# The first block of x in two halves, one on each hardware DMA queue

## The chip, the cores and the metric

The kernel runs on one core of one Trainium2 chip. Times are device microseconds of whole executions: three runs of the kernel before took 225.52, 225.52 and 226.03 us, so the median is 225.52 us. One further execution was taken with the hardware profiler. Its own time is 226.47 us and its span, from the first to the last instruction, is 224.7 us; 1.77 us lie around the span. All rows below are from that execution, and times in them count from the start of its span.

## What is computed

A transformer block over S = 2048 rows (tokens) of width D = 512, in bfloat16. `x` is layer-normalised once, and two branches are added to it:

```
xn  = layernorm(x)                                    # no scale, no shift
out = x + A(xn) + B(xn)

A:  q, k, v = split(xn @ wqkv)                        # 32 heads of 16
    each row s attends to rows s, s-2, ..., s-14      # 8 keys, dilation 2
    A = concat(softmax(q k / 4) v) @ wo

B:  z  = gelu(xn @ w_in)                              # width 1792, two halves of 896
    z1, z2 = z[:, :896], layernorm(z[:, 896:])
    g  = w_sp @ z2 + b_sp                             # mixes the 2048 rows
    B  = (z1 * g) @ w_out
```

## The kernel before

The 2048 rows are 16 blocks of 128 rows, one row per partition. A block of `x` is 128 x 512 bfloat16, 128 KB, in one of eight slots `("xin", slot)`. For a block, `ln_block` (from L664) issues bn_stats on VectorE (L668), bn_aggr (L671), the power that gives the reciprocal deviation on GpSimd (L673), and the normalised block (L686). Blocks 0 to 3 are then transposed by TensorE against an identity matrix (L702) and copied out of PSUM by ScalarE (L709); blocks 4 to 15 are transposed by a DMA on SP's queue (L690).

Block 0 takes a shorter way. As soon as its mean is known, its columns 256 to 511 are centred on VectorE (L676, `ctr1`) and its columns 0 to 255 on ScalarE (L678, `ctr0`, with the sign turned, which an identity with -1 takes back). TensorE transposes these (`xTr0b`, then `xTr0a`), and the product with the second half of `w_in` (`z2_0_...`, L913) begins on them; the division by the deviation is put into the gelu that reads the product (L920).

The columns 896 to 1791 of `w_in`, which `z2` needs, come in four loads (L611) of 224 KB: `w_in2a` and `w_in2b` are the two column halves, and `_0` and `_1` are rows 0 to 255 and 256 to 511. The `_0` loads are on SP's queue, the `_1` loads on ScalarE's. Block 0's product takes the rows of `_1` first.

Each engine has a list of task names in `plan.orders`, written out by hand, that fixes the order of its work; a planner puts semaphores between tasks according to what each reads and writes. The lists begin so:

```
TensorE: warm xTr0b fill0 xTr0a fill1 z2_0_0b z2_0_1b xTr1a xTr1b z2_0_0a z2_0_1a z2_1_0a ...
ScalarE: actprime ldw_in2a_1 ldw_in2b_1 ldx2 ctr0 xTe0b xTe0a xTe1a ...
VectorE: zeros steps0 steps1 bnst0 bnag0 ctr1 bnst1 bnag1 ctrB norm0 bnst2 bnag2 norm1 bnst3 norm2 ...
SP:      ldx0 ldx1 ldw_in2a_0 ldw_in2b_0 ldx3 ldx4 ldx5 ldx6 ldk ldx7 ldx10 ldx8 ldq ldx11 xTd4 ...
```

`warm` is 29 matmuls of 146 columns on constants (L640), ahead of everything else on TensorE; `fill0` and `fill1` are one and three more. `ldx4`, `ldx5`, `ldx6`, `ldx7`, `ldk` and `ldq` are made to wait until `ldw_in2b_1` has landed. `xTd4` and so on are the DMA transposes. After the first four blocks come the projections to q and k (L756), the rest of `z2` (L890) and `z1` (L933), the projection to v (L740), the mixing product with `w_sp` (L1051), and the output products (L1258, L1262).

Of the kernel before, what the change touches and what calls it, by code (L numbers as in the profile page):

```python
# [328 lines left out]
def build_kernel(nc, A_x, A_wqkv, A_wo, B_x, B_w_in, B_w_sp, B_b_sp, B_w_out, out, report=False, sched_kw=None,  # L329
# [14 lines left out]
    x2 = A_x[0]  # L344
# [75 lines left out]
    with ExitStack() as es:  # L420
# [137 lines left out]
        def dma(eng, fn, nbytes, chan, reads=(), writes=(), name="", xbar=False, prio=None, lat=1700.0):  # L558
            return T(eng, fn, reads=tuple(reads), writes=tuple(writes), name=name, prio=prio,
                     dma=dict(chan=chan, nbytes=nbytes, xbar=xbar, lat=lat))  # L560
# [10 lines left out]
          name="steps0")  # L571
        T("dve", lambda v: v.memset(FCa(foff["st6"] + 8, [[9, NB], [1, 1]]), LN_EPS * D), writes=["st_eps"], est=160,
          name="steps1")
# [5 lines left out]
          writes=["ident"], est=350, name="ident1")  # L579
# [3 lines left out]
          writes=["nident"], est=350, name="nident1")  # L583
        T("pool", lambda g: g.memset(AC(off["KT"], [[KW, 4], [1, KP]]), 0.0),
          writes=[("KTpad", c, 0) for c in range(4)], est=200, name="ktpad", prio=2)
# [15 lines left out]
        def xin_ap(sl):  # L601
            return A("xin", 512, 512 * sl) if sl < 4 else A("xin2", 512, 512 * (sl - 4))

        def ld_x(b, eng="sp", after=()):
            sl = b % 8
            dma(eng, lambda e: e.dma_start(xin_ap(sl), x2[128 * b:128 * b + 128, :]), 128 * 512 * 2,
                ("xin", sl), reads=after, writes=[("xin", sl)], name="ldx%d" % b)
# [7 lines left out]

        ld_x(0)
        ld_x(1)
# [4 lines left out]
        for which, eng in ((0, "sp"), (1, "sp")):  # L622
# [4 lines left out]
                writes=[(("wq", "wk")[which], c) for c in range(4)],  # L627
                name="ld%s" % ("qk"[which]))
# [7 lines left out]
        def filler(n, name, est, prio=None, reads=(), w=512):  # L636
# [10 lines left out]
          est=-1200, name="actprime", tbl="gelu")  # L647
# [16 lines left out]
        def ln_block(b):  # L664
            sl = b % 4
            xs_ = b % 8
            xin = xin_ap(xs_)
            T("dve", lambda v: v.bn_stats(Fv("st6", 6, 9 * b), xin),  # L668
              reads=[("xin", xs_)], writes=[("st6", b)],
              est=690, name="bnst%d" % b)  # L670
            T("dve", lambda v: v.bn_aggr(Fv("mv", 2, 2 * b), Fv("st6", 9, 9 * b)), reads=[("st6", b), "st_eps"],  # L671
              writes=[("mv", b)], est=180, name="bnag%d" % b)
            T("pool", lambda g: g.tensor_tensor(Fv("rstd", 1, b), Fv("mv", 1, 2 * b + 1), Fv("mhalf", 1), ALU.pow),  # L673
              reads=[("mv", b), "mhalf"], writes=[("rstd", b)], est=580, name="rstd%d" % b)
            if b == 0:
                T("dve", lambda v: v.tensor_scalar(A("attn", 256, 256), xin[:, 256: 512], Fv("mv", 1, 2 * b), None, ALU.subtract),  # L676
                  reads=[("xin", xs_), ("mv", b)], writes=[("xc", 1)], est=250, name="ctr1")
                T("act", lambda a: a.activation(A("attn", 256), xin[:, 0: 256], ACTF.Identity, bias=Fv("mv", 1, 2 * b),  # L678
                                                scale=-1.0),
                  reads=[("xin", xs_), ("mv", b)], writes=[("xc", 0)], est=400, name="ctr0")  # L680
            if b == 1:
# [3 lines left out]
            xk = "xn0" if b == 0 else ("xn", sl)  # L685
            T("dve", lambda v: v.tensor_scalar(AC(xo, [[1, 512]]), xin, Fv("mv", 1, 2 * b),  # L686
                                               Fv("rstd", 1, b), ALU.subtract, ALU.mult),
              reads=[("xin", xs_), ("mv", b), ("rstd", b)], writes=[xk], est=400, name="norm%d" % b)
            if b >= XDMA:
# [588 lines left out]
        for t in range(NT):  # L1278
# [11 lines left out]
            if t >= 1:  # L1290
# [17 lines left out]
            """  # L1308
                actprime ldw_in2a_1 ldw_in2b_1 ldx2 ctr0 xTe0b xTe0a xTe1a xTe1b z2g0_0 z2g0_1 xTe2a xTe2b xNe xTe3a
                xTe3b z2g1_0 xNeB z2g1_1 z2g2_0 z2g3_0 z2g3_1 z2g2_1 QKe0_0 z2s0 QKe0_1 QKe0_2 QKe0_3 z2s1 QKe1_0 z2s2  # L1310
# [33 lines left out]
            """  # L1344
                ldx0 ldx1 ldw_in2a_0 ldw_in2b_0 ldx3 ldx4 ldx5 ldx6 ldk ldx7 ldx10 ldx8 ldq ldx11 xTd4 xTd5 xTd6 xTd7
                ldx9 ldx14 ldx13 ldx12 xTd10 xTd11 ldx15 xTd8 xTd9 ldwv xTd14 ldb xTd12 xTd13 xTd15 ldw_in1 w0_1 w0_0
# [56 lines left out]
```

## Time and profile before

| | |
|---|---|
| three runs | 225.52, 225.52, 226.03 us |
| profiled execution, its own time | 226.47 us |
| its span | 224.7 us |
| TensorE busy | 220.6 us, 98% of the span |
| VectorE busy | 207.8 us, 92% |
| ScalarE busy | 135.0 us, 60% |
| GpSimd busy | 89.7 us, 40% |
| moved by DMA | 29.96 MB, 133 GB/s on average |

In the rows, PE is TensorE, PEld its weight loads, DVE VectorE, ACT ScalarE, POOL GpSimd. SPq and ACTq are the DMA-issuing instructions of SP and ScalarE. "L913 PE MATMUL ... x10" is ten matmuls of line 913 that follow each other; the first number is the start of the first one, the second the time until the last one ends. A matmul's end is modelled, and the next one starts before it. In the chain of work, each piece is followed back to what released it, and the pieces follow each other without overlap.

### The profile page before, as it was taken

What the parts mean: (1) busy time and instruction counts of PE and PEld (TensorE: products, weight loads), DVE (VectorE), ACT (ScalarE), POOL (GpSimd) and SP (SyncE); (2) the same over time, 40 slices, a digit from 0 to 9 for tenths busy, and PEclk for the clock granted to TensorE, in tenths of its full rate; (3) what the DMA queues carried; (4) which work ended last, traced back from release to release, by engine and by line L of the source; (5) the groups of instructions that cost most, each with busy time, mean ns of one, the idle gap of its engine ahead of it and who ended that gap; (6) DMA issues with size and microseconds to landing.
All of it is one profiled execution on the core that took longest, in us unless ns stands there. A gap on an engine that the chain in (4) does not pass through costs nothing.

```text
span 224.7 us, 3133 instructions
## 1 busy us (share of the span) xinstructions
PE 220.6 (98%) x1170; PEld 123.3 (55%) x1184; DVE 207.8 (92%) x237; ACT 135.0 (60%) x242; POOL 89.7 (40%) x38
## 2 busy tenths in 40 slices
PE   8999999999999999999999999999999999999995
PEld 7555555554577776665555454544545444444544
DVE  4798999999999999999999999999999999999810
ACT  4679899999999999986343304424404216224442
POOL 3454568985000081000000799955999910000000
PEclk9999999999999999999999999999999999999999
DMA  6895442590000002879779997849989697328352
GB/s 218 266 171 140 94 119 50 122 263 13 3 0 0 0 0 46 213 179 204 183 141 179 228 148 154 180 127 179 187 165 221 137 171 175 98 61 176 111 113 93
DMA packets 77716, 29.96 MB, mean 133 GB/s; under 512 B 68731, under 2 KB 75401, under 8 KB 77702
## 3 DMA queue, kind: packets, MB, share of 16 engines
q1 hardware_dynamic: 74566, 25.08, 55.3%
q10 hardware_dynamic: 3136, 4.69, 6.3%
q8 instruction: 9, 0.15, 0.3%
q14 instruction: 5, 0.04, 0.1%
HBM read 9.05 MB, written 2.10 MB: 50 GB/s over the span
## 4 chain that ended last, share of the span: by engine, by line
PE 97%; DMA 1%; DVE 1%; issue 0%; ACT 0%
PE ps L1051 38%; PE ps L756 12%; PE ps L933 11%; PE ps L1262 11%; PE ps L890 8%; PE ps L740 6%; PE ps L1258 6%; PE ps L913 3%; DMA arena<-in_A_x_dram 1%; PE ps L814 1%; PE ps L702 1%; DVE fpool L668 0%; PE ps L640 0%; PE ps L724 0%; DVE arena L676 0%
## 5 line engine op out<-in xcount | busy, mean ns | idle before, releaser
L1051 PE MATMUL ps<-arena 128*128 128x448 f16 (+1 forms) x448 | 86.7, 352 | 0.0
L873 POOL TENSOR_TENSOR arena<-arena,fpool 128x128 bf16<-128x128 f32 x2 | 49.9, 24944 | 45.7 <-DVE arena L869 45.7
L1051 PEld LDWEIGHTS ps<-arena 128*128 128x128 f16 (+1 forms) x448 | 43.8, 98 | 41.4
L779 DVE TENSOR_TENSOR arena<-arena 128x8192 bf16<-128x8192 bf16 (+1 forms) x10 | 35.6, 3556 | 0.8 <-ACT arena L764 0.8
L1196 DVE TENSOR_TENSOR arena<-arena 128x4096 bf16<-128x4096 bf16 x16 | 36.2, 2282 | 0.0
L962 POOL TENSOR_TENSOR fpool<-fpool 128x4 f32<-128x4 f32 x4 | 18.1, 4538 | 27.3 <-DVE fpool L959 27.3
L756 PE MATMUL ps<-arena 128*128 128x512 bf16 x124 | 27.7, 379 | 0.2
L1200 DVE TENSOR_TENSOR arena<-arena 128x4096 bf16<-128x4096 bf16 (+1 forms) x16 | 27.9, 1745 | 0.0
L1066 ACT ACTIVATE ps<-ps 128x448 f32<-128x448 f32 x16 | 8.4, 527 | 32.2 <-PE ps L1051 24.7
L1262 PE MATMUL ps<-arena 128*128 128x512 bf16 (+2 forms) x125 | 27.1, 355 | 0.1
L787 DVE TENSOR_TENSOR arena<-arena 128x4096 bf16<-128x4096 bf16 (+1 forms) x9 | 26.9, 2992 | 0.1
L933 PE MATMUL ps<-arena 128*128 128x448 bf16 x128 | 24.7, 352 | 0.0
L673 POOL TENSOR_TENSOR fpool<-fpool 128x1 f32<-128x1 f32 x16 | 17.5, 1094 | 17.0 <-DVE fpool L671 16.7
L1069 ACT ACTIVATE arena<-ps,fpool 128x448 bf16<-128x448 f32 x16 | 10.0, 636 | 22.6 <-PE ps L1051 22.6
L933 PEld LDWEIGHTS ps<-arena 128*128 128x128 bf16 x128 | 18.5, 144 | 5.9
L756 PEld LDWEIGHTS ps<-arena 128*128 128x128 bf16 x128 | 14.5, 113 | 13.0 <-issue 0.2
L1271 ACT ACTIVATE arena<-ps 128x512 bf16<-128x512 f32 (+2 forms) x17 | 9.4, 563 | 16.7 <-PE ps L1262 16.7
L890 PE MATMUL ps<-arena 128*128 128x448 bf16 x96 | 19.2, 353 | 0.0
L1262 PEld LDWEIGHTS ps<-arena 128*128 128x128 bf16 x126 | 11.9, 98 | 12.4
L764 ACT ACTIVATE arena<-ps 128x1024 bf16<-128x1024 f32 x16 | 16.1, 1026 | 2.5 <-PE ps L756 2.4
L1258 PE MATMUL ps<-arena 128*128 128x512 bf16 (+2 forms) x65 | 15.3, 353 | 0.4
L945 ACT ACTIVATE arena<-arena 128x896 bf16<-128x896 bf16 x16 | 15.3, 955 | 0.0
(87 smaller groups left out, 260.1 us busy)
## 6 DMA issues: line engine op xcount, KB each, us to landing
arena<-in_A_x_dram ACTq DMA_DIRECT2D x8, 256.0 KB, 3.3
arena<-in_A_x_dram SPq DMA_DIRECT2D x15, 128.0 KB, 2.5
out_dram<-arena ACTq DMA_DIRECT2D x7, 256.0 KB, 2.4
arena<-in_A_wqkv_dram SPq DMA_DIRECT2D x3, 512.0 KB, 4.3
arena<-in_B_w_in_dram SPq DMA_DIRECT2D x1, 896.0 KB, 5.4
arena<-in_B_w_out_dram SPq DMA_DIRECT2D x1, 896.0 KB, 5.1
arena<-arena SPq DMA_DIRECT2D x2, 448.0 KB, 4.5
arena<-arena SPq DMA_DIRECT2D x1, 672.0 KB, 5.6
```

The source lines that it names most:

```text
L756: last = t.matmul(bank(k + which), AC(off["wqk"] + 1024 * dc + col0, [[4, 128]]), AC(off["xnT"] + dc * S + 512 * j, [[1, 512]]), start=(dc ...
L779: T("dve", lambda v: v.tensor_tensor(pbv, qb, kb, ALU.mult), reads=[(t_, c, j) for t_ in ("QT", "KT", "KTpad") for c in cs], writes=[("pb" ...
L787: T("dve", lambda v: v.tensor_tensor(av, av, bv, ALU.add), reads=[("pb", s_) for s_ in b], writes=[("pb", s_) for s_ in a], est=c_dve(4096 ...
L873: T("pool", lambda g: g.tensor_tensor(Rv, Zv, FCa(foff["mone"], [[0, 128]]), ALU.pow), reads=[kz, "mone"], writes=[kr], est=20000, name="s ...
L890: last = t.matmul(ps[:, 512 * (k + hf): 512 * (k + hf) + HF], AC(off["xnT"] + dc * S + 128 * b, [[1, 128]]), AC(off["w_in2"] + FH * dc + H ...
L933: lastm = t.matmul(ps[:, 512 * (k + hf): 512 * (k + hf) + HF], AC(off["xnT"] + dc * S + b, [[NTOK, 128]]), AC(off["w_in1"] + FH * dc + HF ...
L962: T("pool", lambda g: g.tensor_tensor(Fv("rstd2", 4, 4 * j), Fv("msq", 4, 4 * j), mhalf, ALU.pow), reads=[("msq", j), "mhalf"], writes=[(" ...
L1051: last = t_.matmul(pb_(k_), st(k), mv(k), start=(start and k == 0), stop=(k == 7), skip_group_check=True)
L1196: T("dve", (lambda iv, tv, av: lambda v: v.tensor_tensor(tv, iv, av, ALU.mult))(iv, tv, av), reads=[("attn", q // 4)] + [("V", i_) for i_ ...
L1200: T("dve", (lambda n: lambda v: v.tensor_tensor(AC(off["Vs"], [[4096, 2], [1, n]]), AC(off["Vs"], [[4096, 2], [1, n]]), AC(off["Vs"] + n, ...
L1258: t_.matmul(po, AC(off["OT"] + 1024 * (t % 3) + 512 * r_ + 128 * cc, [[1, 128]]), AC(off["wo"] + 512 * cc + c0, [[1, n]]), start=False, st ...
L1262: last = t_.matmul(po, AC(off["z1"] + FH * tb + 128 * fc, [[1, 128]]), AC(off["w_out"] + 512 * fc + c0, [[1, n]]), start=False, stop=(fc = ...
```

## The change

Block 0 of `x` is no longer one load of 128 rows on SP's queue. It becomes two loads of 64 rows, 64 KB each: `ldx0a`, rows 0 to 63, stays first on SP's queue, and `ldx0b`, rows 64 to 127, goes to ScalarE's queue, ahead of the two weight loads there. Each half has its own semaphore, and what reads block 0 depends on both.

```
-        ld_x(0)
+        for h in range(2):
+            dma(("sp", "act")[h], (lambda h: lambda e: e.dma_start(xin_ap(0)[64 * h: 64 * h + 64, :], x2[64 * h: 64 * h + 64, :]))(h),
+                64 * 512 * 2, (("xin", 0), "xin0b")[h], writes=[(("xin", 0), "xin0b")[h]], name="ldx0%s" % "ab"[h])
         ld_x(1)
...
             T("dve", lambda v: v.bn_stats(Fv("st6", 6, 9 * b), xin),
-              reads=[("xin", xs_)], writes=[("st6", b)],
+              reads=[("xin", xs_)] + (["xin0b"] if b == 0 else []), writes=[("st6", b)],
...
     plan.orders, ScalarE:
-                actprime ldw_in2a_1 ldw_in2b_1 ldx2 ctr0 xTe0b xTe0a xTe1a ...
+                actprime ldx0b ldw_in2a_1 ldw_in2b_1 ldx2 ctr0 xTe0b xTe0a xTe1a ...
     plan.orders, SP:
-                ldx0 ldx1 ldw_in2a_0 ldw_in2b_0 ldx3 ...
+                ldx0a ldx1 ldw_in2a_0 ldw_in2b_0 ldx3 ...
```

`ctr1`, `ctr0` and `norm0` also name `xin0b` among what they read. The order of all other instructions on all engines stays what it was.

More of the change, by code (lines that the diff above doesn't have):

```diff
@@ L676, in ln_block @@
                 T("dve", lambda v: v.tensor_scalar(A("attn", 256, 256), xin[:, 256: 512], Fv("mv", 1, 2 * b), None, ALU.subtract),
-                  reads=[("xin", xs_), ("mv", b)], writes=[("xc", 1)], est=250, name="ctr1")
+                  reads=[("xin", xs_), "xin0b", ("mv", b)], writes=[("xc", 1)], est=250, name="ctr1")
                 T("act", lambda a: a.activation(A("attn", 256), xin[:, 0: 256], ACTF.Identity, bias=Fv("mv", 1, 2 * b),
                                                 scale=-1.0),
-                  reads=[("xin", xs_), ("mv", b)], writes=[("xc", 0)], est=400, name="ctr0")
+                  reads=[("xin", xs_), "xin0b", ("mv", b)], writes=[("xc", 0)], est=400, name="ctr0")
             if b == 1:
@@ L687, in ln_block @@
                                                Fv("rstd", 1, b), ALU.subtract, ALU.mult),
-              reads=[("xin", xs_), ("mv", b), ("rstd", b)], writes=[xk], est=400, name="norm%d" % b)
+              reads=[("xin", xs_), ("mv", b), ("rstd", b)] + (["xin0b"] if b == 0 else []), writes=[xk], est=400, name="norm%d" % b)
             if b >= XDMA:
@@ L1308, in build_kernel @@
             """
-                actprime ldw_in2a_1 ldw_in2b_1 ldx2 ctr0 xTe0b xTe0a xTe1a xTe1b z2g0_0 z2g0_1 xTe2a xTe2b xNe xTe3a
+                actprime ldx0b ldw_in2a_1 ldw_in2b_1 ldx2 ctr0 xTe0b xTe0a xTe1a xTe1b z2g0_0 z2g0_1 xTe2a xTe2b xNe xTe3a
                 xTe3b z2g1_0 xNeB z2g1_1 z2g2_0 z2g3_0 z2g3_1 z2g2_1 QKe0_0 z2s0 QKe0_1 QKe0_2 QKe0_3 z2s1 QKe1_0 z2s2
@@ L1344, in build_kernel @@
             """
-                ldx0 ldx1 ldw_in2a_0 ldw_in2b_0 ldx3 ldx4 ldx5 ldx6 ldk ldx7 ldx10 ldx8 ldq ldx11 xTd4 xTd5 xTd6 xTd7
+                ldx0a ldx1 ldw_in2a_0 ldw_in2b_0 ldx3 ldx4 ldx5 ldx6 ldk ldx7 ldx10 ldx8 ldq ldx11 xTd4 xTd5 xTd6 xTd7
                 ldx9 ldx14 ldx13 ldx12 xTd10 xTd11 ldx15 xTd8 xTd9 ldwv xTd14 ldb xTd12 xTd13 xTd15 ldw_in1 w0_1 w0_0
```

## The prediction

> **What bounds the kernel now.** I read the page's busy times first, then the chain of work, then the chain in order of time, where the share of each engine can be put into a place.
>
> ```profile
> PE 220.6 (98%) x1170; PEld 123.3 (55%) x1184; DVE 207.8 (92%) x237; ACT 135.0 (60%) x242; POOL 89.7 (40%) x38
> ...
> PE 97%; DMA 1%; DVE 1%; issue 0%; ACT 0%
> ```
>
> ```profile
> 0.74 0.07 issue
> 0.80 2.55 DMA arena<-in_A_x_dram
> ...
> 3.38 0.70 DVE fpool L668
> ...
> 4.11 0.21 DVE fpool L671
> ...
> 4.34 0.30 DVE arena L676
> 4.63 0.14 issue
> 4.77 0.37 PE ps L702 x2
> ...
> 5.93 1.26 PE ps L913 x4
> 7.19 0.22 PE ps L702 x4
> 7.42 1.89 PE ps L913 x10
> ...
> 13.61 0.05 issue
> 13.66 10.74 PE ps L756 x49
> ```
>
> From 4.77 us to the end the chain is TensorE alone, with pieces of 0.05 us between. Only the first 4.77 us are something else: the load of block 0 (2.55 us from its issue at 0.80), then bn_stats, bn_aggr and the centring on VectorE. The change works on that head. What it can take away is therefore bounded by the load's part of 4.77 us, and everything behind must move forward with it.
>
> Two things stand between an earlier load and an earlier end. The first is what TensorE does meanwhile; the second is its pace. The timeline of the first microseconds, TensorE and the DMA issues:
>
> ```profile
> 0.84 3.69 PE L640 MATMUL ps<-const-bfloat16-1.0 128*128 128x146 bf16 x29 [0.84 <-PEq L1388]
> 4.77 0.37 PE L702 MATMUL ps<-arena 128*128 128x128 bf16 x2 [0.24 <-DVE arena L676]
> 4.93 0.42 PE L640 MATMUL ps<-const-bfloat16-1.0 128*128 128x256 bf16 x1
> ...
> 5.72 1.47 PE L913 MATMUL ps<-arena 128*128 128x448 bf16 x4
> ...
> 7.25 2.06 PE L913 MATMUL ps<-arena 128*128 128x448 bf16 x10
> ```
>
> ```profile
> 0.80 0.88 SPq L606 DMA_DIRECT2D arena<-in_A_x_dram  x2
> ...
> 0.94 0.95 ACTq L611 DMA_DIRECT2D arena<-in_B_w_in_dram  x2
> ...
> 1.72 0.95 SPq L611 DMA_DIRECT2D arena<-in_B_w_in_dram  x2
> ...
> 1.92 0.49 ACTq L606 DMA_DIRECT2D arena<-in_A_x_dram  x1
> ```
>
> The 29 filler matmuls stand ahead of block 0 in TensorE's order and last until 4.53 us by their modelled end; TensorE is idle for only 0.24 us before the first transpose. Whatever the load gains beyond about that is spent waiting for the fillers. A next matmul may start before the modelled end of the last (L640 at 4.93, 0.21 us ahead of 4.77 + 0.37), so I put this cap at 0.24 to 0.45 us.
>
> As to the pace: the first L913 matmuls follow each other at 0.37 us (the 1.47 us of four, less one's overlap, and 1.26 / 4 = 0.315 in the chain, where the step is inside), the next ten at 1.89 / 10 = 0.189 us. The form is the same, so TensorE doubles its pace at about 6.9 us, though the page prints a granted clock of full speed in every slice. If that step keeps its place in time, an earlier start by s buys only s / 2, because the time won is spent at half pace.
>
> **What the load of block 0 waits for.** Busy time in stretches of 0.5 us; the last two columns are the DMA engines' busy share and GB/s:
>
> ```profile
> 1.50:2.00 0.50, 0.50 (x6) 0.50 (x5) 0.00 (x0) 0.50 (x1) 0.35 (x3) 1.00 0.21 66
> 2.00:2.50 0.50, 0.50 (x7) 0.50 (x6) 0.00 (x0) 0.29 (x2) 0.24 (x2) 1.00 0.75 203
> 2.50:3.00 0.50, 0.50 (x7) 0.50 (x6) 0.00 (x0) 0.00 (x0) 0.00 (x0) 1.00 0.91 273
> 3.00:3.50 0.50, 0.50 (x7) 0.50 (x6) 0.12 (x1) 0.00 (x0) 0.00 (x0) 1.00 1.08 373
> ```
>
> By 2.5 us 0.5 x (66 + 203) = 134 thousand bytes have moved, as much as block 0 holds, but block 0 lands only at 3.35. So part of what moved was not block 0: its tail shares the DMA engines with the first weights on ScalarE's queue, issued 0.14 us after it. What a load of this size takes with emptier engines shows in block 4's, issued at 5.5 us:
>
> ```profile
> L606 SPq DMA_DIRECT2D arena<-in_A_x_dram x1: 340/340/340, 5.5 to 5.5; - x1
> ...
> DMA to landing us min/median/max: 2.0/2.0/2.0
> ```
>
> **The change, part by part.** *The first half on SP.* It has the place of the whole load (issue at 0.80 us) and half its packets, so it lands no later than 3.35 us; it isn't the later half, and costs nothing. Its issue is one instruction as before (0.88 / 2 = 0.44 us), so SP's next loads keep their times.
>
> *The second half on ScalarE's queue.* It takes the first place there, at 0.94 us. No row shows a load of 64 rows. Bounds: with block 4's 2.0 us it lands at 2.94; with block 0's own 2.55 us, as crowded as now, at 3.49, which is 0.14 us later than today. I take 3.05 us, close to the first, because the weights that crowded the load are now behind it on its own queue, and only block 1 on SP's queue (issued 0.44 us behind the first half) can get between. That is 0.30 us earlier. Bn_stats, bn_aggr and centring follow at their own durations, with VectorE idle before them, so they move by the same 0.30.
>
> *TensorE.* The first transpose moves by the smaller of 0.30 and the cap; I take 0.27. The centring on ScalarE and the copies out of PSUM move along, as ScalarE is idle there. At half pace until about 6.9 us that is 0.13 us of gain, at full pace 0.27.
>
> *ScalarE's other loads.* One more issue of 0.95 / 2 = 0.48 us stands ahead of `w_in2a_1`, `w_in2b_1` and block 2. Their times to landing, in this order:
>
> ```profile
> L611 ACTq DMA_DIRECT2D arena<-in_B_w_in_dram x1: 432/432/432, 0.9 to 0.9; - x1
> ...
> DMA to landing us min/median/max: 3.0/3.0/3.0
> ```
>
> ```profile
> L611 ACTq DMA_DIRECT2D arena<-in_B_w_in_dram x1: 488/488/488, 1.4 to 1.4; - x1
> ...
> DMA to landing us min/median/max: 4.1/4.1/4.1
> ```
>
> ```profile
> L606 ACTq DMA_DIRECT2D arena<-in_A_x_dram x1: 489/489/489, 1.9 to 1.9; - x1
> ...
> DMA to landing us min/median/max: 4.3/4.3/4.3
> ```
>
> They land at 3.9, 5.5 and 6.2 us now, and at most 0.48 us later then: 4.4, 6.0 and 6.7. The first is needed by the first L913, at 5.72 - 0.27 = 5.45: cover 1.0 us. The second is needed by the third L913, two matmuls of 0.37 later: 6.2 us, cover 0.2 us, the thinnest on TensorE. The third feeds the third bn_stats, which has no cover at all:
>
> ```profile
> 6.21 0.69 DVE L668 BATCH_NORM_STATS2 fpool<-arena 128x6 f32<-128x512 bf16 x1
> ...
> 7.95 0.40 DVE L686 TENSOR_SCALAR arena<-arena,fpool 128x512 bf16<-128x512 bf16 x1
> ...
> 18.15 2.29 DVE L779 TENSOR_TENSOR arena<-arena 128x4096 bf16<-128x4096 bf16 x1 [0.82 <-ACT arena L764]
> ```
>
> ```profile
> L702 PE MATMUL ps<-arena x4: 219/219/219, 9.1 to 9.3; 128*128 128x128 bf16 x4
> ```
>
> VectorE then runs up to 0.5 us late: block 2 is normalised at 8.35 + 0.5 = 8.85 us, and TensorE transposes it at 9.1 - 0.2 = 8.9: just covered. VectorE's lateness ends at 18.15 us, where it waits 0.82 us for ScalarE today.
>
> *SP's later loads* wait for `w_in2b_1`:
>
> ```profile
> SPq L606 <- DMA arena<-in_B_w_in_dram: 2.4, 1, 2.4
> ```
>
> Blocks 4 to 7 and the weights of q and k come up to 0.5 us later. Block 4 lands at 5.5 + 2.0 = 7.5 us and is wanted by VectorE only behind block 3's work, after the L686 row of 7.95, so 0.5 is about covered. I cost it at nothing.
>
> **The sum**, against the profiled execution's own 226.47 us (1.77 us around the span don't change): 226.47 - 0.13 to 0.27 = 226.2 to 226.34. The three runs have their median 0.95 us below the profiled execution; the same difference taken from the median gives 225.52 - 0.13 to 0.27. I say **225.35 us**, 0.1% less. Under 0.3% (0.68 us) a measurement of this kernel can't be told from no change.
>
> **A rule of the skill against the change.** The trace shows both queues in flight at once: the weights that ScalarE issued at 0.94 land at 3.9, block 0 at 3.35. The Trainium skill, DMA: Bandwidth & Descriptors, Rules for kernel authors, says of two transfers to disjoint halves of the partitions that one should not bother: both spread over the same 16 DMA engines and serialise. By that rule splitting alone wins nothing; the rows leave room for the other part, the place ahead of the weights.
>
> **The rivals.** *No gain.* The halves finish no sooner than the whole did. For it: the same engines serve both queues, and block 1 follows the first half on SP's queue as the weights followed before. Against: 0.21 and 0.75 busy shares while block 0 moves. Landing at 3.49 it costs 0.14 us at full pace, 0.07 at half: 225.6 us.
>
> *A larger gain, through the pace.* The 0.24 us gap before the first transpose closes; if the step in pace comes with unbroken work, it comes earlier. Had it come where the fillers end, at 4.53 instead of 6.9 us, 2.4 us at half pace would be 1.2 us less, plus the full 0.27: 224.1. Halfway, 224.7. For it: the runs differ by 0.51 us among themselves, as a step that isn't tied to the program would make them. Against: that gap didn't prevent the step now. The Trainium skill, TensorE: Matmul & The Clock Gate, The HAM clock gate, says that the clock doubles after a busy window of about 3.4 us and that this window runs free of the kernel. By that rule the gap hardly matters and the step's place is chance; the trace agrees in the doubling, and one execution can't show the rest.
>
> *Slower: a hole in TensorE's work just before the step.* `w_in2b_1` lands after 6.2 us, because SP's queue has weights of its own in flight from 1.72 us on. By itself the wait costs what it lasts, 0.3 us where it lands at 6.5, as SP's second weight load does today. It decides only where the hole delays the step in pace: the fillers took 6.9 - 0.84 = 6.1 us of work to reach it, so the price runs from half the hole to half of 6.1 us, 3.0 us; in the middle 1.5 us: 226.9 us. For it: cover of 0.2 us only. Against: part of the DMA traffic ahead of it is lighter by the half that left SP's queue.
>
> **How the numbers follow.** Forecast (225.1 to 225.5) 0.46; no gain (225.5 to 225.7) 0.18; larger gain through the pace (224.1 to 224.9) 0.20; slower 0.16. The first two and the spread of the runs (225.52 to 226.03) fall within 0.3%, but for a little: faster 0.22, same 0.62, slower 0.16. The range leaves out the slower case and the lower end of the larger gain: 224.5 to 226.1 us; for the forecast alone 225.0 to 225.8.
>
> **What would show it.** In the profile after: the wait of L668 for block 0 shorter by 0.3 us (1.97 us now); TensorE's idle time before its first L702 gone or below 0.1 us; the first L913 at about 5.45 us; third bn_stats later than 6.21 us and nobody on TensorE waiting for it; the pace still doubling near 6.9 us. The prediction is wrong if block 0 lands at 3.35 or later, if L913 waits for a weight load, or if the step in pace moves.

## The result, and the profile after

Eleven runs of the changed kernel have their median at 227.23 us (lowest 227.04), eleven runs of the kernel before beside them at 225.87 us (lowest 225.38). The ratio is 1.0074, with a 95% interval of 1.0049 to 1.0099: the change makes the kernel 0.7% slower, where 0.1% faster was predicted. Two of the eleven runs (228.88 and 228.90 us), and three of the six of e14 below (229.43 to 229.77), had a granted clock of 0.992 to 0.993 and took some 1.7 us longer than the others; without them the medians are 227.22 us here, 0.6% above the kernel before, and 227.72 us in e14. The profiled execution took 227.11 us, with a span of 225.4 us; before, these were 226.47 and 224.7.

In the page, the shares of the chain that ended last have moved. Only the first row of that part is shown:

```profile
PE 93%; DMA 2%; ACT 1%; DVE 1%; ACTq 1%; issue 0%
```

Before, 97% was TensorE. The chain in order of time (start, duration, what) shows what came in:

```profile
1.52 0.78 ACTq L611
...
2.34 0.49 ACTq L611
...
2.86 4.70 DMA arena<-in_A_x_dram
...
7.58 0.70 DVE fpool L670
...
9.40 0.33 DVE arena L688
9.72 0.05 issue
9.77 0.40 PE ps L704 x4
...
14.29 0.81 PE ps L758 x3
```

The chain no longer starts with block 0. It goes through the two weight issues on ScalarE's queue to the load of block 2, issued at 2.86 us, which takes 4.70 us to land at 7.56. The third bn_stats (L670, before: L668) starts at 7.58, and the third group of transposes (L704, before: L702) at 9.77. Before, the same three stood at 6.2, 6.21 and 9.15. The projections (L758, before: L756) start at 14.29 instead of 13.66: 0.63 us, and the spans differ by 0.7.

TensorE and VectorE in their timelines (in brackets the idle time before, and what ended it):

```profile
4.71 0.40 PE L704 MATMUL ps<-arena 128*128 128x128 bf16 x2 [0.19 <-DVE arena L678]
...
6.01 0.78 PE L915 MATMUL ps<-arena 128*128 128x448 bf16 x2
6.94 0.55 PE L915 MATMUL ps<-arena 128*128 128x448 bf16 x2 [0.15 <-DMA arena<-in_B_w_in_dram]
7.33 0.39 PE L704 MATMUL ps<-arena 128*128 128x128 bf16 x4
7.55 2.06 PE L915 MATMUL ps<-arena 128*128 128x448 bf16 x10
9.77 0.40 PE L704 MATMUL ps<-arena 128*128 128x128 bf16 x4 [0.16 <-DVE arena L688]
```

So the first transpose is 0.06 us earlier (4.71, before 4.77), the first product is 0.29 us later (6.01, before 5.72), and two waits have appeared, one for `w_in2b_1` at 6.94 and one for block 2 at 9.77. TensorE's waits in the first 14 us add a third, of its weight loads, for the first product:

```profile
PEld ps L915 <- DMA arena<-in_B_w_in_dram: 0.8, 1, 0.8
```

The lateness begins with the issues of SP and ScalarE (start, duration):

```profile
0.80 0.59 SPq L617 DMA_DIRECT2D arena<-in_A_x_dram  x1
1.45 0.56 SPq L606 DMA_DIRECT2D arena<-in_A_x_dram  x1
2.06 0.95 SPq L611 DMA_DIRECT2D arena<-in_B_w_in_dram  x2
```

```profile
0.94 0.55 ACTq L617 DMA_DIRECT2D arena<-in_A_x_dram  x1
1.52 0.79 ACTq L611 DMA_DIRECT2D arena<-in_B_w_in_dram  x1
2.34 0.49 ACTq L611 DMA_DIRECT2D arena<-in_B_w_in_dram  x1
2.86 0.49 ACTq L606 DMA_DIRECT2D arena<-in_A_x_dram  x1
```

A half takes 0.59 and 0.55 us to issue, where the whole of block 0 and the first weights took 0.40 and 0.43. The next weight issue takes 0.79. ScalarE's three loads are therefore issued 0.58, 0.93 and 0.94 us later than before (1.52, 2.34 and 2.86 against 0.94, 1.41 and 1.92), and SP's weights 0.34 us later (2.06 against 1.72). What the halves themselves got for it shows in the view of their line (times from issue to landing):

```profile
L617 ACTq DMA_DIRECT2D arena<-in_A_x_dram x1: 547/547/547, 0.9 to 0.9; - x1
...
DMA to landing us min/median/max: 2.2/2.3/2.4
```

One half lands 2.2 us after 0.80, the other 2.4 us after 0.94, at 3.3. The whole block landed at 3.35. Nothing was won there: bn_stats for block 0 starts at 3.41 us (3.38 before). In the trace it starts 0.10 us behind the later half's landing, at 3.31; before, it started 0.02 us behind the landing. So it is in all executions below: 0.10 us where block 0 comes in two loads, 0.02 where it comes in one, and the few hundredths that the halves win are lost in this. And the DMA engines started late. Stretches of 0.5 us as in the prediction, the last number GB/s:

```profile
1.50:2.00 0.50, 0.50 (x6) 0.50 (x5) 0.00 (x0) 0.50 (x1) 0.35 (x3) 1.00 0.00 0
2.00:2.50 0.50, 0.50 (x7) 0.50 (x6) 0.00 (x0) 0.29 (x2) 0.24 (x2) 1.00 0.44 135
2.50:3.00 0.50, 0.50 (x7) 0.50 (x6) 0.00 (x0) 0.00 (x0) 0.00 (x0) 1.00 0.86 225
3.00:3.50 0.50, 0.50 (x7) 0.50 (x6) 0.09 (x1) 0.00 (x0) 0.00 (x0) 1.00 1.00 226
3.50:4.00 0.50, 0.50 (x7) 0.50 (x5) 0.50 (x1) 0.00 (x0) 0.00 (x0) 1.00 0.81 156
...
4.50:5.00 0.50, 0.31 (x4) 0.25 (x4) 0.50 (x2) 0.38 (x1) 0.50 (x1) 1.00 1.08 369
5.00:5.50 0.50, 0.50 (x7) 0.48 (x5) 0.46 (x2) 0.35 (x1) 0.07 (x1) 1.00 1.10 380
```

Before, the first four of these moved at 66, 203, 273 and 373 GB/s, and the fifth was:

```profile
3.50:4.00 0.50, 0.50 (x7) 0.50 (x6) 0.50 (x1) 0.00 (x0) 0.00 (x0) 1.00 1.13 372
```

The late start is the smaller part: by 2.5 us 0.07 MB are missing, and 0.18 MB more from 3.0 to 4.0 us. The DMA view from 1.5 to 5 us adds it up, first for the kernel before, then for the changed one:

```profile
DMA packets 1143, 1.00 MB, mean 285 GB/s; under 512 B 75, under 2 KB 1143, under 8 KB 1143
```

```profile
DMA packets 815, 0.70 MB, mean 200 GB/s; under 512 B 70, under 2 KB 815, under 8 KB 815
```

By 5 us 0.30 MB less has come in. At the 369 to 380 GB/s that the changed kernel moves from 4.5 us on, that is 0.8 us by which the stream of first loads is behind. Block 2 and `w_in2b_1` are later than that, by 1.4 us: on ScalarE's queue 64 KB more stand ahead of them. At half of 375 GB/s these would take 0.35 us, an estimate; the rest isn't explained.

### The profile page after: what moved, and what is told of

Its sections match the earlier page's. It is cut to its first block, busy times and chain, and to the rows that moved or that the text cites. A ratio compares the mean times of both kernels' runs of the same rounds, so it can differ in the third digit from the quotient of the medians.

```text
span 225.4 us, 3135 instructions
## 1 busy us (share of the span) xinstructions
PE 220.9 (98%) x1170; PEld 122.9 (55%) x1184; DVE 207.8 (92%) x237; ACT 135.0 (60%) x242; POOL 89.7 (40%) x38
## 3 DMA queue, kind: packets, MB, share of 16 engines
q10 hardware_dynamic: 3216, 4.75, 6.4%
## 4 chain that ended last, share of the span: by engine, by line
PE 93%; DMA 2%; ACT 1%; DVE 1%; ACTq 1%; issue 0%
PE ps L1053 38%; PE ps L758 12%; PE ps L935 11%; PE ps L1264 11%; PE ps L892 8%; PE ps L742 6%; PE ps L1260 6%; DMA arena<-in_A_x_dram 2%; PE ps L816 1%; PE ps L915 1%; DVE fpool L670 1%; ACTq L611 1%; ACT arena L922 1%; ACT L648 0%; PE ps L704 0%
## 5 line engine op out<-in xcount | busy, mean ns | idle before, releaser
L758 PE MATMUL ps<-arena 128*128 128x512 bf16 x124 | 27.7, 379 | 0.2
L758 PEld LDWEIGHTS ps<-arena 128*128 128x128 bf16 x128 | 14.5, 113 | 13.0
```

The lines of the kernel that those rows point to most:

```text
L758: last = t.matmul(bank(k + which), AC(off["wqk"] + 1024 * dc + col0, [[4, 128]]), AC(off["xnT"] + dc * S + 512 * j, [[1, 512]]), start=(dc ...
```

## The experiments

Where the profiles had left the question: TensorE waits both for `w_in2b_1` (call it W: the loss is made by late weights) and for block 2 (call it X: the loss is made by late x), and either could come from the issue at the head of ScalarE's queue, from the 64-row form, or from the bytes on the shared engines. The first four kernels take the parts of the change one at a time, the next four tell W from X, the next four price block 2 and other orders, the last three ask whether late data is all there is. Ratios are to runs of the kernel before on the same chip; e8 and e15 are single runs. In the table (e13 and e14 are in the text), "projections" is the start of the first projection matmul in the profiled execution, "rest" is its span less that start.

| run | median us | ratio to before, 95% | first transpose | projections | span | rest |
|---|---|---|---|---|---|---|
| before (prediction's) | | | 4.77 | 13.66 | 224.7 | 211.0 |
| e8 before again | one, 226.10 | | 4.79 | 13.08 | 224.4 | 211.3 |
| after | 227.23 | 1.0074 [1.0049, 1.0099] | 4.71 | 14.29 | 225.4 | 211.1 |
| e15 after again | one, 226.96 | | 4.75 | 14.14 | 225.2 | 211.1 |
| e1 both halves on SP | 227.37 | 1.0062 [1.0050, 1.0074] | 5.78 | 14.56 | 225.6 | 211.0 |
| e2 whole at ScalarE's head | 227.55 | 1.0060 [1.0043, 1.0077] | 4.74 | 14.73 | 225.9 | 211.2 |
| e3 half of block 1 there | 226.70 | 1.0043 [1.0028, 1.0058] | 4.40 | 13.76 | 224.8 | 211.0 |
| e4 4 KB there | 226.84 | 1.0039 [1.0025, 1.0053] | 4.33 | 14.52 | 225.6 | 211.1 |
| e5 after, no w_in2 needed | 227.29 | 1.0056 [1.0042, 1.0069] | 4.75 | 14.27 | 225.6 | 211.3 |
| e6 before, no w_in2 needed | 226.06 | 1.0008 [0.9995, 1.0020] | 4.65 | 14.06 | 225.4 | 211.3 |
| e7 block 1 and weights exchanged | 225.85 | 0.9994 [0.9983, 1.0006] | 4.68 | 12.81 | 224.1 | 211.3 |
| e9 blocks 2 and 3 exchanged | 226.34 | 1.0025 [1.0014, 1.0035] | 4.68 | 13.52 | 224.6 | 211.1 |
| e10 halves by columns | 226.81 | 1.0045 [1.0031, 1.0059] | 4.32 | 14.32 | 225.6 | 211.3 |
| e11 as e5, block 2 first | 227.08 | 1.0055 [1.0033, 1.0076] | 4.78 | 14.20 | 226.2 | 212.0 |
| e12 block 2 and weights exchanged | 226.19 | 1.0012 [1.0003, 1.0021] | 4.70 | 13.48 | 224.6 | 211.1 |

The last column is the main reading: but for e11 the rest is 211.0 to 211.3 us, whatever was done to the first loads. What differs between these kernels is over by the first projection, and all of it is when TensorE gets there. The first transpose's column doesn't go with it. Each of these columns is one execution, and the kernel before alone has its projections at 13.08 and at 13.66; a single row of them proves little, and the ratios rest on the medians. Nor can a difference under 0.3 us in the projections be read as one in time, as the rest varies by that much.

**e1: the split without the second queue.** Both halves on SP's queue, ScalarE's as before.

```
-            dma(("sp", "act")[h], ... ldx0a/ldx0b
+            dma("sp", ...
     ScalarE:  actprime ldw_in2a_1 ldw_in2b_1 ldx2 ...
     SP:       ldx0a ldx0b ldx1 ldw_in2a_0 ldw_in2b_0 ldx3 ...
```

> Both halves of block 0 on SP's queue, one behind the other; ScalarE's queue as in the kernel before. Theory Q (the extra load at the head of ScalarE's queue pushes the first weights back, which leaves holes in TensorE's work): the weights on ScalarE's queue land near 3.9 and 5.5 us again, the first L915 is at 5.7 us, and the time is within 0.3% of the kernel before. Theory H (a load of 64 rows is itself dear to issue, 0.55 to 0.59 us against 0.40, and starts the transfers late): SP's loads come 0.8 us later than before, block 0 lands no sooner than 3.3 us, and the time is 0.3 to 0.7% above the kernel before.

The issues take 576 and 592 ns, with 128 rows' 398 before. The weights are in time, but the second half of block 0 lands 2.9 us after its issue, at 4.4:

```profile
L617 SPq DMA_DIRECT2D arena<-in_A_x_dram x2: 576/584/592, 0.8 to 1.4; - x2
...
DMA to landing us min/median/max: 2.6/2.7/2.9
```

The first transpose moves to 5.78 us. H has its time, and Q's "within 0.3%" failed. So the split alone, with no load added to ScalarE's queue, costs as much as the change, by another route: on one queue the second half is late, on two queues everything else is.

**e2: the move without the split.** Block 0 whole, 128 rows, at the head of ScalarE's queue; SP begins with block 1.

```
-        ld_x(0)
+        ld_x(0, "act")
     ScalarE:  actprime ldx0 ldw_in2a_1 ldw_in2b_1 ldx2 ...
     SP:       ldx1 ldw_in2a_0 ldw_in2b_0 ldx3 ...
```

> Block 0 whole (128 rows) at the head of ScalarE's queue; SP starts with block 1. No load of 64 rows. Theory Q: 128 KB and one issue ahead of the weights on ScalarE's queue; w_in2a_1 lands at 5 us or later, w_in2b_1 at 6.3 us or later, 0.4 to 0.8% slower than the kernel before. Theory H: issues of 0.4 to 0.49 us, transfers start at 1.85 to 2.0 us, the weights land at most 0.5 us later than before (4.4 and 6.0), within 0.3% of the kernel before.

Issues of 128 rows take 0.38 to 0.40 us on both queues. Block 0 is no earlier, and TensorE waits for `w_in2b_1`:

```profile
7.37 0.55 PE L913 MATMUL ps<-arena 128*128 128x448 bf16 x2 [1.20 <-DMA arena<-in_B_w_in_dram]
```

The loss is the same size as the change's without any 64-row load, as Q expected and H didn't: a load put ahead of the first weights is enough. But in this execution the stream is hardly behind: 0.95 MB have moved by 5 us, against 1.00 before. The trace has 16 increments of a semaphore for each of these loads, and the last one is the landing. Fifteen of `w_in2b_1`'s come by 6.25 us and the last at 7.32; of block 2's, by 6.87 and at 8.00. One part in sixteen is late here, not all.

**e3 and e4: what one more issue there costs.** In e3 block 0 stays whole on SP, and the second half of block 1 takes the place at ScalarE's head. In e4 a load of 4 KB that is needed late (`b_sp`) takes it.

```
e3   ScalarE:  actprime ldx1b ldw_in2a_1 ldw_in2b_1 ldx2 ...      SP:  ldx0 ldx1a ...
e4   ScalarE:  actprime ldb ldw_in2a_1 ldw_in2b_1 ldx2 ...        SP:  ldx0 ldx1 ... (ldb left out)
```

> Block 0 stays whole and first on SP's queue; block 1 is split instead, its second half at the head of ScalarE's queue. Block 0 no longer plays a part in the split. Theory Q: w_in2a_1 lands after 5 us, w_in2b_1 after 6.5 us, 0.4 to 0.8% slower than the kernel before, like the change. Theory H: SP's first issue is 0.40 us again and only ScalarE's is 0.55 us; transfers start at 1.83 us; slower by 0.2 to 0.4%.

> The kernel before with a load of 4 KB (b_sp, which SP loads later otherwise) at the head of ScalarE's queue: one more issue there, next to no bytes. Theory Q in its pure form (the issue alone counts): weights 0.45 us later or more, w_in2a_1 at 4.4 us or later, and 0.2 to 0.5% slower. If it is the bytes ahead of the weights, or the 64 rows, that count: w_in2a_1 lands by 4.5 us and the time is within 0.2% of the kernel before.

Both get block 0 early, which the change was to do and didn't: with the first weights issued 0.58 and 0.42 us later, the whole load of 128 rows lands at 3.1 and 3.0 us, without being split. The first transposes follow at 4.40 and 4.33 without idle time before them, at the cap that the fillers set. Both are still 0.4% slower, as Q had it, though e3's weights land at 4.8 and 6.0 us, earlier than Q expected. In e3:

```profile
6.06 0.55 PE L915 MATMUL ps<-arena 128*128 128x448 bf16 x2 [0.34 <-DMA arena<-in_B_w_in_dram]
...
9.24 0.40 PE L704 MATMUL ps<-arena 128*128 128x128 bf16 x4 [0.43 <-DVE arena L688]
```

Even 4 KB ahead of the weights costs 0.9 us (it comes in small packets, 204 under 512 B by 5 us against 75 before, so this isn't the price of an issue alone). An earlier block 0 is worth nothing as long as the loads behind it are late.

**e5 and e6: W against X.** In both, the product (L915, before: L913) of blocks 0 to 3 reads a tile of zeros where it read `w_in2`, so that it doesn't wait for the weights; e5 does that to the changed kernel, e6 to the one before.

```
-   t.matmul(ps[...], st, AC(off["w_in2"] + FH * dc + c0, [[1, HF]]), ...
-   reads=[..., (wk_, h)]
+   t.matmul(ps[...], st, A("zeros", HF), ...
+   reads=[..., "zeros"]
```

> The changed kernel, but the z2 products of blocks 0 to 3 (L915) read a tile of zeros, which is ready at 1.2 us, in place of the columns of w_in that the four first weight loads bring; these loads are still issued, and all other work is as it was (the output's z2 of these blocks is not computed). So L915 can't wait for a weight load. Theory W (the late weights make the loss): the time falls to the kernel before or below, at most 0.2% above it. Theory X (block 2 of x, late behind the weights on ScalarE's queue, makes the loss through the third bn_stats and the third transpose): the wait of L704 for VectorE near 9.7 us stays, grows to about 0.8 us, and the kernel stays 0.4% or more slower than the kernel before.

> The same edit in the kernel before, as the control (z2 of blocks 0 to 3 is not computed from w_in). No theory has TensorE waiting for the weights there, so the time is that of the kernel before within 0.2%. If it is faster by 0.3% or more, the weights held TensorE before the change as well.

The wait for weights is gone in e5, and the time is not better: 1.0056. TensorE is ahead and gives it all back before the third transposes, for which block 2 isn't there (TensorE, then VectorE):

```profile
6.50 2.06 PE L915 MATMUL ps<-arena 128*128 128x448 bf16 x10
9.96 0.40 PE L704 MATMUL ps<-arena 128*128 128x128 bf16 x4 [1.40 <-DVE arena L688]
```

```profile
7.77 0.69 DVE L670 BATCH_NORM_STATS2 fpool<-arena 128x6 f32<-128x512 bf16 x1 [1.52 <-DMA arena<-in_A_x_dram]
```

So W isn't needed for the loss, and X is sufficient. The control is unchanged in time (1.0008). Its profiled execution happens to be the slowest of its twelve, 227.09 us against the median of 226.06, and shows the same hole from the other side: there block 2 came late by itself, third bn_stats at 7.57 us after a wait of 1.41 us, and TensorE waited 1.29 us. A late block 2 thus costs about 1 us in a kernel without the change too. Its loads and their issues are those of the kernel before, and 0.95 MB have moved by 5 us. What is late is again one part: fifteen of block 2's increments come by 5.82 us, as in the prediction's profile (5.86), and the last at 7.54 instead of 6.19. Meanwhile the DMA share (the number before the last) is about one engine in sixteen:

```profile
6.50:7.00 0.50, 0.50 (x6) 0.23 (x3) 0.00 (x0) 0.50 (x2) 0.00 (x0) 1.00 0.07 25
7.00:7.50 0.50, 0.50 (x4) 0.27 (x3) 0.00 (x0) 0.50 (x2) 0.00 (x0) 1.00 0.07 23
```

In the changed kernel it is different: all sixteen increments of block 2 come from 6.74 to 7.56 us, the first of them later than the last before. Why a part falls behind in e2 and e6, no run here shows.

**e7: an order that should keep both in time.** Block 1 heads ScalarE's queue, and `w_in2a_1` goes behind block 0 on SP's.

```
     ScalarE:  actprime ldx1 ldw_in2b_1 ldx2 ...
     SP:       ldx0 ldw_in2a_1 ldw_in2a_0 ldw_in2b_0 ldx3 ...
```

> The kernel before with two loads exchanged one for one: block 1 heads ScalarE's queue, and w_in2a_1 follows block 0 on SP's. The number of issues on each queue stays. If block 0's load is held up by what heads the other queue, block 0 lands at 3.0 to 3.2 us instead of 3.35 and TensorE's first transpose is at 4.4 to 4.6 us instead of 4.77. By the theory that an extra issue on ScalarE's queue makes the loss, nothing is lost: w_in2b_1 lands at 5.5 us, block 2 at 6.2 us, time equal or 0.1 to 0.2% faster. If the bytes ahead of each load decide, w_in2a_0 and w_in2b_0 land 0.3 us later, still in time.

Block 0 lands at 3.27 (3.0 to 3.2 was expected of a load that is held up by the other queue's first), and the third bn_stats is at 6.28: nothing late, nothing won, 0.9994. It adds no issue to either queue, and it is the only reordering here that costs nothing.

**e8: the kernel before, once more.**

> The kernel before once more, for a second trace. If the landing times are set by the program, block 0 lands at 3.35 us within 0.1, the weights at 3.9 to 6.6 us within 0.2, and block 2 at 6.2 us. If the step in TensorE's pace falls at another moment, the span differs by up to 1 us with the same landings.

With the same order and the same loads, four products now take 1.08 us where they took 1.47 in the prediction's profile, and the projections start at 13.08 instead of 13.66:

```profile
5.75 1.08 PE L913 MATMUL ps<-arena 128*128 128x448 bf16 x4
```

The doubling of TensorE's pace comes some 0.7 us earlier, at about 6.1 us instead of 6.8. The execution took 226.10 us, 0.37 less than the prediction's 226.47, about half of 0.7. So a late step is part of why the medians differ by 1.36 us and the two first profiles by only 0.64, and not all of it. The landings weren't all where they were expected: block 0's was, at 3.4, but `w_in2b_1` landed at 4.9 us instead of 5.5 and block 2 at 5.8 instead of 6.2.

**e9: block 2 late alone.** Blocks 2 and 3 exchange queues, so that block 2 comes last on SP's.

```
     ScalarE:  actprime ldw_in2a_1 ldw_in2b_1 ldx3 ...
     SP:       ldx0 ldx1 ldw_in2a_0 ldw_in2b_0 ldx2 ldx4 ...
```

> The kernel before with blocks 2 and 3 of x exchanged between the queues: block 2 is the last of SP's first loads (block 3 landed there at 6.9 us), block 3 is on ScalarE's queue. Block 0 and all weights as before. It measures the price of block 2's lateness alone. Theory X (block 2 sets the end): it lands 0.7 us later, at 6.9 us, TensorE's third transpose waits for VectorE by 0.3 to 0.7 us and the kernel is 0.15 to 0.35% slower (0.3 to 0.8 us). If block 2's landing doesn't matter below 7.5 us: within 0.1% of the kernel before.

Here nothing is split and nothing added. Block 2 is 0.6 us later than in the prediction's profile:

```profile
6.81 0.69 DVE L668 BATCH_NORM_STATS2 fpool<-arena 128x6 f32<-128x512 bf16 x1 [0.71 <-DMA arena<-in_A_x_dram]
```

TensorE waits 0.42 us before the third transposes, and the median is 226.34 against 225.77, 0.57 us. The late block has the price that X gives it.

**e10: the halves by columns.** Both halves have 128 rows of 512 bytes, on the two queues, in the change's order.

```
-   xin_ap(0)[64 * h: 64 * h + 64, :],      x2[64 * h: 64 * h + 64, :]
+   xin_ap(0)[:, 256 * h: 256 * h + 256],   x2[0:128, 256 * h: 256 * h + 256]
```

> The change with another cut: each half is all 128 rows and half of the columns (512 bytes a row), on the same queues at the same places. Theory H (64 rows are dear to issue): the two issues take 0.40 us instead of 0.55 to 0.59, transfers start at 1.85 us instead of 2.1, block 2 lands at 6.6 to 7.0 us instead of 7.56, and the kernel is 0.2 to 0.45% slower than the kernel before instead of 0.6 to 0.75%. If the extra load on ScalarE's queue alone makes the loss: the same landings and time as the change, 0.6% or more.

With 128 rows an issue of 64 KB takes 0.39 and 0.38 us, and both halves have landed 1.9 and 2.0 us after it:

```profile
L617 ACTq DMA_DIRECT2D arena<-in_A_x_dram x1: 384/384/384, 0.9 to 0.9; - x1
...
DMA to landing us min/median/max: 1.9/2.0/2.0
```

Block 0 is complete at 2.9 us, 0.4 us earlier than whole: in this form the step that was predicted does happen, the first transpose is at 4.32, and the kernel is 0.45% slower all the same. Most of that step needs no halves: in e4, with the weights as late, the whole load lands at 3.0. TensorE waits 0.36 and 0.25 us for weights and 0.61 us for block 2. H has its issues and its time, but not its reason: block 2 lands at 7.6 us, as in the change, and not at 6.6 to 7.0, and 0.73 MB have moved by 5 us. The halves of 512-byte rows have the stream as late as the halves of 64 rows.

**e11: the changed kernel with block 2 in time.** As e5, with block 2 directly behind the second half on ScalarE's queue, ahead of the weights that aren't needed there.

```
     ScalarE:  actprime ldx0b ldx2 ldw_in2a_1 ldw_in2b_1 ...
```

> The changed kernel with the tile of zeros in place of w_in's first columns (z2 of blocks 0 to 3 is not computed from w_in), as in e5, and block 2 issued on ScalarE's queue right behind block 0's second half, ahead of the weights that nothing waits for now. Theory X: block 2 lands at 5 us or sooner, the wait of the third transpose goes, and the time falls from 0.56% above the kernel before to within 0.2% of it. If something else in the change makes the loss, the time stays 0.4% or more above.

The expectation from X failed. Block 2 is in time (third bn_stats at 6.21 us), and the time is still 1.0055 (the profiled execution, 227.96 us, is the slowest of the six, whose median is 227.08). The loss has moved to what now comes last: block 3 (VectorE, first row) and, through `w_in2b_1`, which SP's loads of blocks 4 to 7 and of the q and k weights wait for, the projections themselves (TensorE, second and third):

```profile
8.21 0.69 DVE L670 BATCH_NORM_STATS2 fpool<-arena 128x6 f32<-128x512 bf16 x1 [0.80 <-DMA arena<-in_A_x_dram]
```

```profile
9.27 0.40 PE L704 MATMUL ps<-arena 128*128 128x128 bf16 x4 [0.58 <-DVE arena L688]
...
14.20 2.11 PE L758 MATMUL ps<-arena 128*128 128x512 bf16 x9 [0.46 <-DMA arena<-in_A_wqkv_dram]
```

So X names only the first in a row. Several of the first loads are late, and whichever load is put last takes over.

**e12: block 2 ahead in the kernel before.** Block 2 on SP behind block 1, `w_in2a_0` in its place on ScalarE's queue.

```
     ScalarE:  actprime ldw_in2a_1 ldw_in2b_1 ldw_in2a_0 ...
     SP:       ldx0 ldx1 ldx2 ldw_in2b_0 ldx3 ...
```

> A try at a faster kernel: the kernel before with block 2 and w_in2a_0 exchanged between the queues, so block 2 is issued at 1.72 us on SP's queue instead of 1.92 on ScalarE's, with less ahead of it. Theory X: block 2 lands near 5.3 us, w_in2a_0 near 6.2 us, needed at 6.4 to 7.2 us. Where the step in pace is early block 2 was just in time before, so the gain is small: 0 to 0.2% faster. If w_in2a_0 is then late, TensorE waits for it and the kernel is up to 0.2% slower.

Third bn_stats at 6.04 us, but the fourth waits 0.29 us for block 3, and TensorE waits too:

```profile
7.07 2.05 PE L913 MATMUL ps<-arena 128*128 128x448 bf16 x10 [0.39 <-ACT arena L709]
```

The view names ScalarE's copy, but in the kernel before the same products start ahead of that copy (at 7.25 us, the copy at 7.34). What they need here is `w_in2a_0`, issued at 1.9 us, which takes 5.0 us to land. The ratio is 1.0012, as the expectation had it for a late `w_in2a_0`. Time given to block 2 is taken from another load.

**e13 and e14: all blocks early, with and without the change.** As e5 and e6, with all four loads of `w_in2` moved behind the q weights on SP's queue; blocks 4 to 7 and the weights of q and k wait for block 3 instead of `w_in2b_1`.

```
e13  ScalarE:  actprime ldx0b ldx2 ...
     SP:       ldx0a ldx1 ldx3 ldx4 ... ldq ldw_in2a_1 ldw_in2b_1 ldw_in2a_0 ldw_in2b_0 ldx11 ...
e14  ScalarE:  actprime ldx2 ...
     SP:       ldx0 ldx1 ldx3 ldx4 ... ldq ldw_in2a_1 ldw_in2b_1 ldw_in2a_0 ldw_in2b_0 ldx11 ...
```

> The changed kernel with L915 of blocks 0 to 3 reading zeros (those rows of z2 are then not computed), and with every load of w_in2 moved behind the load of the q weights on SP's queue, so that blocks 1, 2 and 3 follow the halves directly; blocks 4 to 7 and the q and k weights wait for block 3 in place of w_in2b_1. Late stream is the whole cause: all blocks land before VectorE wants them, TensorE waits for nobody between its first L704 and the projections, and the time is within 0.3% (0.7 us) of e14's, at or below the kernel before's. Something else of the change costs (the two semaphores, the bn_stats that waits twice, the 64-row form itself): 1.0 to 1.7 us slower than e14, as the change was.

> The control for e13: the same two edits in the kernel before, block 0 whole on SP's queue and block 2 alone on ScalarE's. Late stream: block 0 lands at 3.0 to 3.1 us as in e3 and e4, since no weights run beside it, so the halves have no more than 0.1 to 0.2 us to win here; time at or up to 1 us below the kernel before's, and within 0.7 us of e13. If something else costs, e14 is 1.0 to 1.7 us faster than e13.

Their times are 227.93 us (1.0091 [1.0078, 1.0104]) and 228.66 us (1.0118 [1.0085, 1.0151]). By the 227.72 us given above for e14, the two are 0.2 us apart. Against "something else costs", the split kernel isn't 1.0 us or more behind; against the other theory, neither is at or below the kernel before's time. The reason is a cost that the edit brought in itself: the moved loads push back the DMA transposes on SP's queue, and TensorE waits 1.2 us (e13) and 1.6 us (e14, where the view names no releaser) in the middle of the projections. In e13:

```profile
13.38 6.85 PE L758 MATMUL ps<-arena 128*128 128x512 bf16 x31
21.48 7.10 PE L758 MATMUL ps<-arena 128*128 128x512 bf16 x31 [1.24 <-DMA arena<-arena]
```

Up to that hole the question is answered: TensorE waits for nobody between its first transpose and the projections, which start at 13.38 us with the change and at 13.28 without. Once data is early, the two semaphores and the 64-row form together cost 0.10 us at that point, of the 0.63 us that the change lost there; the rest of the loss in the changed kernel is late data. For the split itself the pair is unkind: with no weights beside it the whole block lands at 3.15 us, the halves at 3.28.

**e15: the changed kernel, once more.**

> The changed kernel once more. Both theories: issue of the 64-row halves 0.55 to 0.60 us, block 0 landing at 3.3, w_in2b_1 and block 2 later than 6.5 us, TensorE waiting for VectorE before the third block's transposes at 9.6 to 9.9 us, and the projections starting at about 14.2 us whether the step in pace comes at 4, 6 or 7 us; time 227.0 to 227.5 us.

Here the pace doubles at about 5.0 us, and TensorE's gain from it ends at once in a wait for `w_in2b_1`:

```profile
5.62 0.55 PE L915 MATMUL ps<-arena 128*128 128x448 bf16 x2
6.94 0.55 PE L915 MATMUL ps<-arena 128*128 128x448 bf16 x2 [0.76 <-DMA arena<-in_B_w_in_dram]
...
9.62 0.40 PE L704 MATMUL ps<-arena 128*128 128x128 bf16 x4
```

The third bn_stats waits 1.17 us, until 7.43. The projections start at 14.14, as expected, against 14.29 with a step some 1.3 us later: data holds the changed kernel, and an early step is worth 0.15 us to it. To the kernel before, a step 0.7 us earlier was worth 0.58 there (13.66 against 13.08) and 0.37 in time. The wait for VectorE ahead of the third transposes, expected here, isn't shown by this execution: block 2 is normalised by 9.56 us, when TensorE has just finished the ten products that the weights held up. W and X each hold TensorE to nearly the same moment. The time, 226.96 us, is just under the expected 227.0.

## Why the prediction was wrong

*What failed first: "They land ... at most 0.48 us later".* The prediction charged ScalarE's queue one more issue and let each landing move by that. This is the term that turned the sign: the lateness of ScalarE's other loads, put at 0.48 us and taken as covered. The issues moved by 0.58 to 0.94 us, as a half issues in 0.55 us and the weights behind it in 0.79. `w_in2a_1`, `w_in2b_1` and block 2 landed at 5.9, 6.9 and 7.56 us, where 4.4, 6.0 and 6.7 were forecast: 1.9, 1.4 and 1.4 us later than before. The prediction took the landings from the issue alone. The runs show two things in its place: the stream of first loads moved 0.30 MB less by 5 us (0.8 us), and 64 KB more stood ahead on that queue. In e2 and e6, one late part in sixteen makes a load late with the stream in time, so bytes aren't the whole account of a landing either.

*"SP's next loads keep their times."* They didn't; a half issues in 0.59 us and SP's weights came 0.34 us later.

*"3.05 us, close to the first".* Block 0 landed at 3.3, inside the bounds of 2.94 and 3.49, but at today's time. The reason given, that the crowding weights are now behind, was right as such: in e3, e4 and e10, with the weights issued later, block 0 does land at 2.9 to 3.1, and in e3 and e4 it is one load. What the bound of block 4's load didn't have in it is the 64-row form: its transfers start later (DMA share 0.00 from 1.5 to 2.0 us, 0.21 before). Nor did the sum have the 0.07 us that bn_stats starts later behind two loads.

*The cap of 0.24 to 0.45 us.* Right: where block 0 was early, the first transposes came at 4.32 to 4.40, 0.37 to 0.45 us ahead of 4.77, without idle time before them.

*"Just covered" and "costed at nothing".* The covers that it found were 1.0, 0.2 and 0.05 us and none; a lateness of 1.4 us goes through all of them. Taken with the measured lateness its own working gives the loss: block 2 normalised at 8.35 + 1.4 = 9.75 us, as measured (9.40 + 0.33), transposes 0.6 us later than before and 0.9 us later than forecast.

*The rival "slower", 226.9 us.* It had the sign, and missed the median by 0.3 us, but not by its mechanism. The wait for `w_in2b_1` it named came (0.15 us, and 0.76 in e15), but the hole didn't delay the step in pace: in both executions the pace had doubled before the hole. Its price is how late the data are, and e5 shows that block 2 alone would have cost as much.

*The pace.* That a step at an unfixed place makes the runs differ is borne out: by rows of the same form it stands at about 6.8 us in the prediction's profile, 6.1 in e8, 5.0 in e15, with the same 29 fillers from 0.84 us ahead of it. The Trainium skill, TensorE: Matmul & The Clock Gate, The HAM clock gate, has the window running free of the kernel, and these places agree with that; a step tied to unbroken work, on which the "larger gain" stood, has nothing for it here: without idle time ahead of the first transposes it stands at 5.1 us in e10 and at 6.3 in e14.

*The rule against the change.* The Trainium skill, DMA: Bandwidth & Descriptors, Rules for kernel authors, has two transfers to disjoint halves of the partitions as not worth the bother, since they share the same engines. The runs agree for halves of 64 rows (block 0 at 3.3 in two queues, 4.4 in one, 3.35 whole). e10's column halves, which landed block 0 0.4 us earlier, aren't what it speaks of; the kernel was slower nevertheless.

What stays open: why a load of 64 rows takes 0.15 to 0.2 us longer to issue than one of 128, why its first bytes move later, and why one part of a load falls behind in e2 and e6. No run here looks into that. How much of the loss is due to the 64-row form isn't settled: e10, without it, loses 0.45%, but its interval overlaps the change's at 1.0049 to 1.0059, and its halves of 512-byte rows bring a late stream of their own.

## What to carry to other kernels

Where a kernel starts on a burst of loads that saturates the DMA engines, price a change by the whole burst: count the bytes moved by a fixed time and divide the shortfall by the rate (0.30 MB at 375 GB/s, 0.8 us), and then ask for every load on both queues whether its cover holds that much. Take it as the least: the loads behind the added one on its own queue were 1.4 to 1.9 us late here, and one late part in sixteen, which the bytes don't show, held loads of e2 and e6 back by 1.1 to 1.9 us. A load that lands just as its reader comes free (6.19 against 6.21 us for block 2) has no cover, and an earlier first load is worth only as much as the last load that isn't early. Kernels that differ in their first microseconds can be compared by the start of the first long stretch of work, but not finer than the rest varies (0.3 us here), and not where the edit reaches past that start (e11, e13, e14).

## What the runs showed of the hardware

- A load of 64 rows takes 0.55 to 0.59 us to issue on either queue (after, e1, e3, e13), one of 128 rows 0.38 to 0.40 as the first of its queue, also where it has only 64 KB (e10). The smaller load is the dearer one, and a load of 128 rows right behind it took 0.56 to 0.79 us (after, e11, e13).
- With a 64-row load at SP's head the DMA engines moved nothing until 2.0 us (share 0.00); before, they were at 0.21 from 1.5 to 2.0.
- With no weights beside it, one load of 128 rows (3.15 us, e14) beat two halves on two queues (3.28, e13).
- A load lands with the last of 16 increments. In e6 fifteen of block 2's came by 5.82 us and the last at 7.54, with the loads and issues of the kernel before.
- bn_stats for block 0 started 0.02 us behind the landing of one load, and 0.10 us behind that of two (six executions with two halves of 64 rows, and e10).
- A load of 4 KB ahead of the first weights (e4) made the kernel 0.4% slower.
- The granted clock was printed as 1.00 from the start in all the profiled executions, while the products of the same form took 0.37 us and then 0.19 us apiece.
